# Decode attention with a gated MLP on one core: shorter ScalarE and VectorE programs, and the last weight load cut 16/8/5/2/1

## The chip, the cores and the metric

The kernel runs on one core of a Trainium2 chip. The metric is the time of one execution on the device in microseconds (us), and smaller is better. The profile's span, from the first to the last instruction, is 1.3 to 1.8 us shorter than that time in the runs of this case.

## The reference

One token attends to a cache of 16,384 keys and values in 32 heads, and a gate mixes the result with a small MLP branch.

```python
g = sigmoid((x * gate_w).sum(-1))                    # x: 1 x 512
q = x @ wq                                           # 32 heads of 128; wq: 512 x 4096
p = softmax(q @ k_cache.T * 128 ** -0.5)             # k_cache: 32 x 16384 x 128, bfloat16
a = (p @ v_cache).reshape(1, 4096) @ wo              # v_cache as k_cache; wo: 4096 x 512
b = (z1 * (w_sp * layernorm(z2) + b_sp)) @ w_out     # z1, z2: halves of gelu(x @ w_in)
return g * a + (1 - g) * b
```

The two caches are 2 x 134.2 MB. Everything else is 11 MB. Each byte is used once.

## The kernel before

Heads are handled in pairs. The whole program hangs on one queue of loads, issued by SyncE (SP) into three buffers of 64 KB per partition in SBUF, the memory next to the engines: wq, w_in and w_out first, then K0, K1, V0, K2, V1, K3, ... V15, then wo.

```python
    k_at = [max(2 * i - 1, 0) for i in range(NP)]          # place of K of pair i in the sequence
    v_at = [min(2 * i + 2, 2 * NP - 1) for i in range(NP)]
    ...
    for n, kind, i in loads:                               # a load waits for its buffer's last user
        wait = [user[n - 3]] if n >= 3 else [w_free] if buf[n % 3] is setup else []
        ...
            sp.op(lambda e, ...: e.dma_start(out=buf[n % 3][...], in_=src[...]), wait=..., inc=(done, 16))
    for j, (a, b) in enumerate(zip(WO_CUTS[:-1], WO_CUTS[1:])):
        sp.op(lambda e, a=a, b=b: e.dma_start(out=wo[:, a * D:b * D], in_=wo_src[:, a * D:b * D]),
              wait=[user[wo_at - 3]] if a == 0 else (), inc=(ld_o[j], 16))
```

For a pair, VectorE (DVE) multiplies K by q, TensorE (PE) adds over the head dimension, DVE finishes the scores, and ScalarE (ACT) takes the exponentials. That frees K's buffer. PE then multiplies V by p, which frees V's.

```python
    def act_pairs(e):
        e.wait_ge(*p_zero)
        exps(e, 0)                       # exps: wait for the scores, two activations
        exps(e, 1)
        with e.Fori(2, NP) as i:
            renew(e)                     # drain PE's sums of an earlier pair, zero the bank
            exps(e, i)
        renew(e)
        ...
```

In the tail the sums are normalized and multiplied by wo: rows 0 to 15 (of 32 per partition) in a loop of four rows, the rest unrolled as the pieces of wo land.

```python
WO_CUTS = (0, 16, 24, 28, 31, 32)
...
    dve.op(lambda e: e.reciprocal(out=rl[:, :], in_=l_ps[:, 0:H]), wait=[(sl_s, 1)], mark=True)
    dve.chain(lambda e: e.tensor_scalar(out=rl, in0=rl, scalar1=g_sb[:, 0:1], ..., op0=ALU.mult, ...))
    o_ok = dve.chain(lambda e: e.tensor_tensor(out=o_sb, in0=o_ps[:, 0:H], in1=rl, op=ALU.mult),
                     wait=[used_v[-1]])
    ...
    for j, (a, b) in enumerate(zip(WO_CUTS[:-1], WO_CUTS[1:])):
        for k in range(max(a, WIDE), b):                   # WIDE = 16
            y_ok = add(o2[:, k:k + 1], wo[:, k * D:(k + 1) * D], [(ld_o[j], 16)] if k == a else (), ...)
        if b == 24:
            add(ones_f[:, 0:1], d_sb[:, :], [w_ok])        # the sum of rows 0 to 15
    # then: copy to SBUF on DVE and ACT, and the DMA of the output
```

The softmax here doesn't subtract the row's maximum and nothing guards it: scores larger than these inputs give would overflow.

## Time and profile before

| | before |
|---|---|
| median of the first three runs | 652.02 us (651.7 to 652.5) |
| span of the profiled run | 650.2 us |
| bytes on the load queue | 279.58 MB, 99.6% of 16 engines' span |
| one 64 KB packet, median of 3,840 | 2.422 us |
| last semaphore of wo's last row | 648.19 us |

The page of the kernel before, its parts 1 to 3 and 4. Part 1 has busy time, share and instructions of each engine; part 2 gives 40 slices of the span; part 3 gives each DMA queue's packets, MB and share of 16 engines' time; part 4 follows the chain that ended last.

```profile
...
PE 424.3 (65%) x2474; PEld 47.0 (7%) x1312; DVE 335.8 (52%) x159; ACT 45.8 (7%) x112; POOL 2.2 (0%) x10
...
GB/s 384 463 419 452 452 395 443 452 443 395 452 452 395 443 452 448 391 452 452 403 435 452 448 391 452 452 431 407 452 452 395 443 452 439 399 435 468 392 428 342
...
q1 hardware_dynamic: 6194, 279.58, 99.6%
q8 instruction: 1, 0.02, 0.0%
...
DMA 4%; SPq 0%; PE 0%; issue 0%; DVE 0%; ACT 0%; ACTq 0%
...
```

No compute engine is busy for more than 65% of the span, and the load queue is busy for 99.6%. That is how a kernel that waits for its bytes reads. The slices, but for the last, swing between 384 and 468 GB/s, since packets of 64 KB are counted whole, where they begin; long stretches are steadier. These are windows of the kernel before; columns are the stretch, its length, busy us (count) of PE, weight loads, DVE, ACT and Pool, the granted clock, the DMA share and GB/s:

```profile
...
40.00:600.00 560.00, 372.78 (x2118) 34.89 (x1069) 307.80 (x122) 32.93 (x89) 0.00 (x0) 0.84 1.00 433
...
647.25:650.20 2.95, 1.19 (x18) 0.50 (x14) 0.41 (x1) 0.36 (x1) 0.00 (x0) 1.00 0.08 24
...
```

The stream runs at 433 GB/s in the middle and is over at 647.25 us, but for 24 GB/s x 2.95 us of stragglers. A 64 KB packet takes 2.422 us, so 16 engines move 16 x 65,536 / 2.422 us = 433 GB/s: the engines are back to back. The Trainium skill, "DMA: Bandwidth & Descriptors", section "Where 436 GB/s comes from", derives a ceiling of 435 GB/s for the fabric, and the measured rate agrees with it; the same section says that the HBM side, at about 358 GB/s, binds loads from HBM, but this trace, of one core alone, shows 433. 279.58 MB at 433 GB/s are 645.7 us of the 650.2.

The rest is the end. These are the last lines of the timeline of the kernel before (start, duration, engine, line, operation, operands, count, and in brackets the idle time before and its releaser):

```profile
...
646.72 0.16 PEld L716 LDWEIGHTS ps_all<-d_sb,const-float32-1.0 128*1 128x1 f32 x4
...
647.02 0.52 PEld L716 LDWEIGHTS ps_all<-bufs,o 128*1 128x1 bf16 x8
...
647.94 0.38 PEld L716 LDWEIGHTS ps_all<-bufs,o 128*1 128x1 bf16 x8 [0.40 <-DMA bufs<-in_A_wo_dram]
...
648.61 0.41 DVE L731 CAST res<-ps_all 1x256 bf16<-1x256 f32 x1 [6.07 <-PE ps_all L716]
...
```

PE finishes the 4-row piece and is idle for 0.40 us until the 3-row piece lands. The 6 matmuls of that piece and the 2 of the last row follow without a wait in between that this view shows. The trace's events of semaphores (counters by which a finished transfer releases the engine that waits for it) are finer: the last row's sixteenth increment came at 648.19 us, and its first weights load at 648.23. (The timeline merges the two stretches because the gap is too short.) The result copy and the output DMA end the kernel.

ACT's timeline of the kernel before:

```profile
...
63.96 1.28 ACT L592 ACT_TABLE_LOAD   x1 [29.56 <-ACTq L86]
65.26 0.42 ACT L592 ACTIVATE p_t<-s_sb 64x256 bf16<-64x256 f32 x1
...
```

The activation table for Exp (1.28 us) is loaded in front of the first exponentials, and K2's load is issued when the first half of them is done.

### The profile page before, as it was taken

Reading aid. Unit: us, or ns where it says so; the run is one execution under the profiler, and the core shown is the slowest. Engines: PE = TensorE matmul, PEld = TensorE weight load, DVE = VectorE, ACT = ScalarE, POOL = GpSimd, SP = SyncE. Lnnn points to the kernel's source line nnn. Section 1 sums busy time; section 2 is a strip of 40 time slices with the busy share of each in tenths; the row PEclk is TensorE's granted clock in tenths of the full one; section 3 lists DMA queues with packets and bytes.
Section 4 is the critical chain, followed back from the end, with each engine's and each line's share of the span. In section 5 each row is a group of like instructions: output and inputs, shape, how many; then the busy total and the mean of one; then the engine's idle time right before and its main releaser. Section 6 shows DMA issues by size and latency. Waiting matters only on the chain. (4 is left out here: it accounts for less than half of the span.)

```text
span 650.2 us, 7753 instructions
## 1 busy us (share of the span) xinstructions
PE 424.3 (65%) x2474; PEld 47.0 (7%) x1312; DVE 335.8 (52%) x159; ACT 45.8 (7%) x112; POOL 2.2 (0%) x10
## 2 busy tenths in 40 slices
PE   0646687847477574857757486584748857478678
PEld 0000000000101000010000101000010100001022
DVE  3457839256380835628165370835628174465600
ACT  2210000100001000010100001000000100001011
POOL 1000000000000000000000000000000000000000
PEclk9959798958889796888969679796977969698979
DMA  9999999999999999999999999999999999999998
GB/s 384 463 419 452 452 395 443 452 443 395 452 452 395 443 452 448 391 452 452 403 435 452 448 391 452 452 431 407 452 452 395 443 452 439 399 435 468 392 428 342
DMA packets 6203, 279.60 MB, mean 430 GB/s; under 512 B 695, under 2 KB 826, under 8 KB 1210
## 3 DMA queue, kind: packets, MB, share of 16 engines
q1 hardware_dynamic: 6194, 279.58, 99.6%
q8 instruction: 1, 0.02, 0.0%
q10 hardware_dynamic: 8, 0.00, 0.0%
HBM read 279.58 MB, written 0.00 MB: 430 GB/s over the span
## 5 line engine op out<-in xcount | busy, mean ns | idle before, releaser
L579 DVE TENSOR_TENSOR bufs<-bufs,qb x64 | 281.4, 4418 | 170.8 <-DVEq L86 170.8
L91 PE MATMUL ps_all<-bufs,ident 128*128 x960 | 258.8, 423 | 0.0
L496 PE MATMUL ps_all<-bufs,ident 128*128 x64 | 28.6, 446 | 154.2 <-PEq L86 153.9
L106 PE MATMUL ps_all<-bufs,p_t 128*8 x1024 | 82.5, 396 | 30.1 <-PEq L86 20.1
L564 DVE TENSOR_REDUCE s_sb<-ps_all 128x64 f32<-128x512 f32 x64 | 44.0, 687 | 93.1 <-DVEq L86 93.1
L91 PE MATMUL ps_all<-zero,ident 128*8 128x512 bf16 (+2 forms) x167 | 59.5, 388 | 0.0
L592 ACT ACTIVATE p_t<-s_sb 64x256 f32 (+1 forms) x32 | 13.3, 415 | 433.1 <-ACTq L86 432.7
L496 PEld LDWEIGHTS ps_all<-bufs,ident 128*128 128x128 bf16 x64 | 6.3, 99 | 365.6 <-issue 365.6
L106 PEld LDWEIGHTS ps_all<-bufs,p_t 128*8 x1024 | 19.4, 83 | 163.1 <-issue 161.6
L531 PE MATMUL ps_all<-pick,d_sb 128*128 128x2 f32 x128 | 17.0, 255 | 16.5 <-PEq L86 16.5
L531 PEld LDWEIGHTS ps_all<-pick,d_sb 128*128 128x128 f32 x128 | 15.7, 193 | 34.7 <-issue 34.7
L601 ACT COPY d_sb<-ps_all 128x512 f32<-128x512 f32 x16 | 9.4, 586 | 105.4 <-ACTq L86 105.4
L606 ACT CAST ps_all<-zero 128x512 f32<-128x512 bf16 x15 | 8.8, 589 | 1.7
L666 DVE RECIPROCAL rl<-ps_all 128x32 f32<-128x32 f32 x1 | 0.4, 357 | 12.2 <-PE ps_all L552 12.2
L381 DVE TENSOR_TENSOR bufs<-ps_all,ident 128x896 f32<-128x896 f32 x2 | 2.1, 1086 | 8.6 <-PE ps_all L91 8.6
L669 DVE TENSOR_TENSOR o_sb<-ps_all,rl 128x32 bf16<-128x32 f32 x1 | 0.2, 191 | 11.5 <-PE ps_all L531 11.5
L592 ACT ACTIVATION_READ_ACCUMULATOR p_t<-s_sb (+1 forms) x32 | 5.9, 185 | 0.0
L321 PE MATMUL ps_all<-xgw,const-float32-1.0 1*128 1x3 f32 x2 | 0.6, 360 | 8.0 <-DVE xgw L317 8.0
L91 PE MATMUL ps_all<-bufs,xb 128*128 x12 | 5.0, 552 | 0.0
L106 PE MATMUL ps_all<-bufs,u 128*1 x14 | 2.6, 372 | 3.1 <-ACT ps_all L427 2.4
L345 PE MATMUL ps_all<-bufs,xb 128*128 x4 | 2.3, 574 | 3.3 <-DMA bufs<-in_B_w_in_dram 3.3
L106 PE MATMUL ps_all<-bufs,xb 128*64 x32 | 3.6, 380 | 0.0
(76 smaller groups left out, 40.2 us busy)
## 6 DMA issues: line engine op xcount, KB each, us to landing
bufs<-in_A_k_cache_dram SPq DMA_DIRECT2D x2, 4096.0 KB, 36.2
bufs<-in_A_v_cache_dram SPq DMA_DIRECT2D x1, 5120.0 KB, 34.5
bufs<-in_A_wq_dram SPq DMA_DIRECT2D x1, 4096.0 KB, 12.3
bufs<-in_A_v_cache_dram SPq DMA_DIRECT2D x1, 2048.0 KB, 39.0
bufs<-in_A_wo_dram SPq DMA_DIRECT2D x1, 2048.0 KB, 25.4
bufs<-in_B_w_in_dram SPq DMA_DIRECT2D x1, 1792.0 KB, 15.5
bufs<-in_A_v_cache_dram SPq DMA_DIRECT2D x1, 1024.0 KB, 41.0
bufs<-in_A_wo_dram SPq DMA_DIRECT2D x1, 1024.0 KB, 27.6
```

Of the source, the lines that this page charges most:

```text
L91: ins = eng.matmul(out, lhsT=lhsT, rhs=rhs, **flags).ins
L106: ins = eng.matmul(bank[0:m, 0:n], lhsT=lhsT, rhs=rhs, **flags).ins
L321: g_ok = pe.op(lambda e: e.matmul(g_ps, lhsT=ones_f[0:1, :], rhs=xgw[:, :], start=True, stop=True), wait=[xgw_ok], mark=True)
L345: if n else matmul_on(nc, e, lambda: e.matmul(args[0], lhsT=args[1], rhs=args[2], **flags), [at, (xa, 0)]))
L381: dve.op(lambda e, h=h, zh=zh: e.tensor_tensor(out=zm[:, 2 * h * ZB:2 * (h + 1) * ZB].rearrange("p (b m k) -> p b m k", b=2, k=FhC), in0=z ...
L496: matmul_on(nc, e, lambda: e.matmul(s3, lhsT=ident[:, :], rhs=k3[:, :, 0:W], start=True, **flags), [(kw, 0)])
L531: ins = e.matmul(o2, lhsT=d_sb[:, r * Dh:(r + 1) * Dh], rhs=pick[:, r * 2:(r + 1) * 2], start=False, stop=False, skip_group_check=True)
L564: return e.tensor_reduce(out=s_sb[:, c * QK:(c + 1) * QK], in_=s_ps[c % 2].rearrange("p (j w) -> p j w", w=W), axis=AX.X, op=ALU.add)
L579: e.tensor_tensor(out=k3, in0=k3, in1=qi, op=ALU.mult).then_inc(mul_s, 1)
L592: e.activation(out=p_t[rows, bass.ds(at, NG * 8)].rearrange("p (t c) -> p t c", c=8)[:, :, 4 * s:4 * s + 4], in_=s_sb[rows, :].rearrange(" ...
L601: return e.copy(out=d_sb[:, :], in_=d_ps)
L606: e.copy(out=d_ps, in_=zero[:, :]).then_inc(drn_s, 1)
```

## The change

The intent: the ScalarE and VectorE programs are shortened, by emitting the exponentials once in a loop of branches and by merging steps of the set-up and of the tail. The last pieces of wo become 5/2/1 rows instead of 4/3/1. The core of the diff:

```diff
-WO_CUTS = (0, 16, 24, 28, 31, 32)
+WO_CUTS = (0, 16, 24, 29, 31, 32)
...
-    for t in [L_sb, p_t, zero]:
+    for t in [sel, L_sb, p_t, zero]:
         p_zero = pool.op(lambda e, t=t: e.memset(t[:, :], 0.0), mark=True)
+    sel_ok = (pool.sem, ident_ok[1] + 1)
-    const_ok = dve.op(lambda e: e.memset(sel[:, :], 0.0), mark=True)
...
-    dve.op(lambda e: e.tensor_copy(out=wbf[:, :], in_=g_ps[:, 1:3]), wait=[gm_ok], mark=True)
-    g_free = dve.chain(lambda e: e.memset(g_ps, 0.0))
+    wbf_ok = act.op(lambda e: e.copy(out=wbf[:, :], in_=g_ps[:, 1:3]), mark=True)
+    g_free = dve.op(lambda e: e.memset(g_ps, 0.0), wait=[wbf_ok], mark=True)
...
     def act_pairs(e):
+        i = counter(e, "ia", 0)
         e.wait_ge(*p_zero)
-        exps(e, 0)
-        exps(e, 1)
-        with e.Fori(2, NP) as i:
+        e.activation(out=var[:, :], in_=eps_t[:, :], func=ACT.Exp)
+        nc.br("act_exps", engines=kind)
+        with nc.body("act_renew", valid_engines=kind):
             renew(e)
-            exps(e, i)
+            nc.br("act_exps", engines=kind)
+        with nc.body("act_exps", valid_engines=kind):
+            exps(e, value(e, i, NP - 1))
+            e.reg_alu(i, i, 1, ALU.add)
+            e.br_lt(i, 2, on_true="act_exps", on_false="act_more")
+        with nc.body("act_more", valid_engines=kind):
+            e.br_lt(i, NP, on_true="act_renew", on_false="act_last")
...
-    dve.chain(lambda e: e.tensor_scalar(out=rl[:, :], in0=rl[:, :], scalar1=g_sb[:, 0:1],
-                                        scalar2=0.0, op0=ALU.mult, op1=ALU.add))
-    o_ok = dve.chain(lambda e: e.tensor_tensor(out=o_sb[:, :], in0=o_ps[:, 0:H], in1=rl[:, :],
-                                               op=ALU.mult), wait=[used_v[-1]])
+    o_ok = dve.chain(lambda e: e.scalar_tensor_tensor(
+        out=o_sb[:, :], in0=o_ps[:, 0:H], scalar=g_sb[:, 0:1], in1=rl[:, :], op0=ALU.mult,
+        op1=ALU.mult), wait=[used_v[-1]])
```

More of the change, by code (lines that the diff above doesn't have):

```diff
@@ L307, in gated_mix_kernel @@
         out=sel[:, :].rearrange("h (i x) -> h i x", x=P + 1)[:, :, 0:P:4],
-        in_=ident[0:H, 0:H].unsqueeze(1).broadcast_to([H, 4, H])), wait=[const_ok, ident_ok],
+        in_=ident[0:H, 0:H].unsqueeze(1).broadcast_to([H, 4, H])), wait=[sel_ok],
         mark=True)
@@ L314, in gated_mix_kernel @@
     dve.op(lambda e: e.tensor_tensor(out=xg_row[:, :], in0=x_row[:, :], in1=gw_row[:, :],
-                                     op=ALU.mult), wait=[(ld_x, 16), (ld_g, 48)], mark=True)
+                                     op=ALU.mult), wait=[(ld_g, 48)], mark=True)
     dve.op(lambda e: e.tensor_copy(out=xgw[:, 1:3], in_=wb_row[:, :]), mark=True)
@@ L324, in gated_mix_kernel @@
            wait=[g_ok], mark=True)
-    gm_ok = act.op(lambda e: e.activation(out=gm_sb[:, :], in_=g_ps[:, 0:1], func=ACT.Sigmoid,
+    act.op(lambda e: e.activation(out=gm_sb[:, :], in_=g_ps[:, 0:1], func=ACT.Sigmoid,
                                           scale=-1.0), mark=True)
-    dve.op(lambda e: e.tensor_copy(out=wbf[:, :], in_=g_ps[:, 1:3]), wait=[gm_ok], mark=True)
-    g_free = dve.chain(lambda e: e.memset(g_ps, 0.0))
+    wbf_ok = act.op(lambda e: e.copy(out=wbf[:, :], in_=g_ps[:, 1:3]), mark=True)
+    g_free = dve.op(lambda e: e.memset(g_ps, 0.0), wait=[wbf_ok], mark=True)
     def pe_gmlp(e):
@@ L608, in act_pairs @@
     def act_pairs(e):
+        kind = [e.engine]
+        i = counter(e, "ia", 0)
         e.wait_ge(*p_zero)
-        exps(e, 0)
-        exps(e, 1)
-        with e.Fori(2, NP) as i:
+        e.activation(out=var[:, :], in_=eps_t[:, :], func=ACT.Exp)
+        nc.br("act_exps", engines=kind)
+        with nc.body("act_renew", valid_engines=kind):
             renew(e)
-            exps(e, i)
+            nc.br("act_exps", engines=kind)
[5 more added lines that the diff above has]
+            e.br_lt(i, NP, on_true="act_renew", on_false="act_last")
+        nc.switch_bb("act_last")
         renew(e)
```

## The prediction

> **What bounds the kernel.** The load stream. The page's queue part gives 279.58 MB on one hardware queue, filling 99.6% of 16 engines' span. In the trace a 64 KB packet takes 2.422 us (median of 3,840), so 16 engines move 65,536 x 16 / 2.422 = 433 GB/s; the windows view shows the same from 40 to 600 us. The Trainium skill, "DMA: Bandwidth & Descriptors", section "Where 436 GB/s comes from", puts the fabric's ceiling at 435 GB/s; the trace agrees. Counting packets in flight, no stretch over 30 ns has fewer than 14 of 16 engines busy between 2.9 and 647.3 us. So 279.58 MB / 433 GB/s = 646 us is fixed by bytes that the change does not touch. About 4 to 5 us at the two ends are left. Compute engines are far below (page, part 1: PE 65%, DVE 52%, ACT 7%).
>
> **What the change does.**
> 1. Set-up. DVE loses the memset of sel (0.27 us) and the copy of wbf (0.16); Pool gains a memset of about 0.3 us and ACT a copy of about 0.2 us (estimates from those). All lie before 17.1 us, where PE waits for w_in's DMA. Worth nothing.
> 2. ScalarE loop. The exponentials are emitted once, not three times; each round adds a compare-and-branch (0.04 us in the trace). A dummy exponential moves the 1.28 us table load from 64.0 us, in front of the first exponentials, to about 34 us. K2's load is issued 1.3 us sooner, but by 65.8 us 31.8 MB had been asked for and about 28 moved (estimate from 433 GB/s): the queue was not empty. Later whole loads take 31 to 41 us from issue to landing (page, part 6) against 19.4 us of their own, so 0.1 us later costs nothing.
> 3. Tail, VectorE. Scale and multiply become one fused multiply: 0.24 us less at 629 us, where 11.5 us of slack follow; the fused one may take 0.05 us more than 0.19 at 641.2 us. PE catches up with the loads after that. Worth nothing.
> 4. wo pieces. The 3-row piece's semaphore comes at 647.91 us and PE resumes at 647.94; the last row's comes at 648.20, its weights load at 648.23. So the last row's landing sets the end already. With 5/2/1 PE has 4 matmuls instead of 6 before the last row, and waits for the same row. Worth 0 to 0.05 us.
> 5. Program length. One 16,384-byte instruction fetch (1.1 us) falls at 647.3 us, amid the last row's stragglers. The Trainium skill, "Runtime: NRT & Kernel Launch", section "Instruction fetch mechanics", says that refills come in 16 KiB blocks; the trace agrees in size. If a shorter program keeps it out of the tail, up to 0.3 us comes off the last landing: one chance in three.
>
> On the critical path: about 0.1 us of 652.
>
> **Prediction.** 651.9 us, range 651.0 to 652.8. Chances: faster by over 2% 0.005, within 2% 0.99, slower 0.005.
>
> **What would show it.** Right: DMA share above 99%, a 64 KB packet at 2.42 us, the chain ending in wo's last pieces, PE, one copy, the output; the table load near 34 us. Step 4 wrong: over 0.1 us between the last row's landing and its matmul, before or after. Step 5 right: no instruction packet, or elsewhere, and a sooner last landing.
>
> **What would make it wrong.** A load issued late because the branch loop delays a buffer's release (a gap in the DMA share); a semaphore or branch stall that the trace of before cannot show; a chip whose stream is slower.

## More of the kernel before

SP's timeline of the kernel before:

```profile
...
65.79 0.33 SPq L638 DMA_DIRECT2D bufs<-in_A_k_cache_dram  x1
90.87 0.33 SPq L638 DMA_DIRECT2D bufs<-in_A_v_cache_dram  x1
```

The line of 90.87 us is V1's load, issued when the first half of the second pair's exponentials is done and K1's buffer is free.

## The result, and the profile after

| | before | after |
|---|---|---|
| median of 6 runs | 651.68 us (651.54 to 652.5) | 651.58 us (651.44 to 653.31) |
| ratio | | 1.0002, 95% interval 0.9989 to 1.0015 |
| span of the profiled run | 650.2 us | 650.2 us |
| wo's last semaphore | 648.19 us | 648.19 us |

The ratio is the mean time of one kernel's fast runs over that of the other's in the same rounds, so it is not quite the ratio of the medians. Here one run of 653.31 us lifts the mean of after while its median is 0.10 us lower.

The page of the kernel after, from the same parts:

```profile
...
PE 423.5 (65%) x2474; PEld 47.0 (7%) x1312; DVE 335.2 (52%) x156; ACT 46.1 (7%) x114; POOL 2.6 (0%) x11
...
q1 hardware_dynamic: 6194, 279.58, 99.6%
q8 instruction: 1, 0.02, 0.0%
...
PE 0%; DVE 0%; issue 0%
...
```

PE is busy for 423.5 us instead of 424.3, DVE for 335.2 instead of 335.8 and ACT for 46.1 instead of 45.8. The load queue has the same bytes and share. Part 4 looks different: before, the chain hung on the DMA of wo, and now it names only PE and DVE. That is a matter of attribution, as the tail shows. Windows of the kernel after:

```profile
...
40.00:600.00 560.00, 372.21 (x2118) 35.16 (x1069) 307.84 (x122) 31.64 (x88) 0.00 (x0) 0.84 1.00 433
...
647.25:650.20 2.95, 1.26 (x18) 0.52 (x16) 0.41 (x1) 0.36 (x1) 0.00 (x0) 1.00 0.05 17
...
```

The end of its timeline:

```profile
...
646.76 0.17 PEld L724 LDWEIGHTS ps_all<-d_sb,const-float32-1.0 128*1 128x1 f32 x4
...
647.28 0.42 PEld L724 LDWEIGHTS ps_all<-bufs,o 128*1 128x1 bf16 x10 [0.36 <-DMA bufs<-in_A_wo_dram]
...
647.96 0.09 PEld L724 LDWEIGHTS ps_all<-bufs,o 128*1 128x1 bf16 x4 [0.26 <-DMA bufs<-in_A_wo_dram]
648.23 0.08 PEld L724 LDWEIGHTS ps_all<-bufs,o 128*1 128x1 bf16 x2 [0.19 <-DMA bufs<-in_A_wo_dram]
...
648.58 0.41 DVE L739 CAST res<-ps_all 1x256 bf16<-1x256 f32 x1 [6.04 <-PE ps_all L724]
...
```

PE stops for the DMA of wo three times after row 24: before the 5-row piece (0.36 us), the 2-row piece (0.26 us) and the last row (0.19 us). The kernel waits for the last landing as before. The followed chain stayed on PE, probably because the matmuls, whose ends are modelled, overlap these waits. From the last semaphore to the copy it is 648.58 - 648.19 = 0.39 us, against 0.42 us before: a gain of 0.03 us.

The other moves of the change, in the kernel after: the early table load and the first exponentials on ACT, the loads that they release on SP, and the fused multiply in DVE's tail, one timeline each.

```profile
...
34.39 1.28 ACT L612 ACT_TABLE_LOAD   x1
35.69 0.20 ACT L612 ACTIVATE var<-eps_t 128x1 f32<-128x1 f32 x1
64.11 0.42 ACT L592 ACTIVATE p_t<-s_sb 64x256 f32 x1 [28.22 <-ACTq L86]
...
```

```profile
...
64.65 0.33 SPq L647 DMA_DIRECT2D bufs<-in_A_k_cache_dram  x1
90.98 0.33 SPq L647 DMA_DIRECT2D bufs<-in_A_v_cache_dram  x1
```

```profile
...
641.17 0.25 DVE L676 SCALAR_TENSOR_TENSOR o_sb<-ps_all,g_sb,rl 128x32 bf16<-128x32 f32 x1 [11.75 <-PE ps_all L531]
...
```

The table load is 29.6 us earlier, and K2's load 1.14 us (64.65 against 65.79). V1's load, one pair later, is not earlier at all (90.98 against 90.87), because the second pair's exponentials wait for the scores. The fused multiply takes 0.25 us. Before, it was 0.24 us for the scaling, long before it was needed, and 0.19 us for the multiply.

### The profile page after: what moved, and what is told of

Its sections match the earlier page's. It is cut to its first block, busy times and chain, and to the rows that moved or that the text cites. A ratio compares the mean times of both kernels' runs of the same rounds, so it can differ in the third digit from the quotient of the medians.

```text
span 650.2 us, 7779 instructions
## 1 busy us (share of the span) xinstructions
PE 423.5 (65%) x2474; PEld 47.0 (7%) x1312; DVE 335.2 (52%) x156; ACT 46.1 (7%) x114; POOL 2.6 (0%) x11
## 5 line engine op out<-in xcount | busy, mean ns | idle before, releaser
L592 ACT ACTIVATE p_t<-s_sb 64x256 f32 x32 | 13.3, 414 | 462.5 <-ACTq L86 462.1
L676 DVE SCALAR_TENSOR_TENSOR o_sb<-ps_all,g_sb,rl 128x32 bf16<-128x32 f32 x1 | 0.3, 251 | 11.7 <-PE ps_all L531 11.7
L592 ACT ACTIVATION_READ_ACCUMULATOR p_t<-s_sb x32 | 5.9, 185 | 0.0
L301 DVE MEMSET ps_all<- 128x3584 f32 x1 | 3.0, 3045 | 1.9 <-PEq L770 1.9
## 6 DMA issues: line engine op xcount, KB each, us to landing
bufs<-in_A_wo_dram SPq DMA_DIRECT2D x1, 2048.0 KB, 25.5
```

The source lines that it names most:

```text
L301: dve.op(lambda e: e.memset(ps_all[:, 0:7 * 512], 0.0), mark=True)
L592: e.activation(out=p_t[rows, bass.ds(at, NG * 8)].rearrange("p (t c) -> p t c", c=8)[:, :, 4 * s:4 * s + 4], in_=s_sb[rows, :].rearrange(" ...
```

## The experiments

Twelve runs of eleven kernels were made, each run a single look beside the kernel before on the same chip (651.54, 652.13 and 651.55 us in the three calls). All passed the comparison with the reference.

Where I speak of "the slowest engine", I read the trace's packet records: a load of 128 packets of 64 KB is spread over 16 DMA engines, and the end of its last packet is the slowest engine's. The Trainium skill, "DMA: Bandwidth & Descriptors", section "Why a DMA increments its semaphore by 16 and not by 1", says that each engine adds its own increment and only the full 16 means that all data has landed. The traces agree: in the kernel after, the last two increments for wo come at 648.19 us, over 0.2 us behind all others, and PE's last weights load at 648.23.

### The cuts alone

```diff
 (on the kernel before)
-WO_CUTS = (0, 16, 24, 28, 31, 32)
+WO_CUTS = (0, 16, 24, 29, 31, 32)
```

> Before, with only the wo cuts of the change (rows 16/8/5/2/1). Theory (the last landing sets the end, and the bytes in front of it are the same): PE stops three times for a wo piece after row 24, at about 647.3, 647.95 and 648.2 us, as in the changed kernel; the last row's weights load at 648.2 us and the result copy starts at 648.55 to 648.62 us, within 0.05 us of before's 648.61. Rival (fewer matmuls behind the next to last landing shorten the tail): the copy starts 0.1 us or more before 648.61.

The end of this kernel's timeline:

```profile
...
648.06 0.09 PEld L716 LDWEIGHTS ps_all<-bufs,o 128*1 128x1 bf16 x4 [0.23 <-DMA bufs<-in_A_wo_dram]
648.35 0.08 PEld L716 LDWEIGHTS ps_all<-bufs,o 128*1 128x1 bf16 x2 [0.21 <-DMA bufs<-in_A_wo_dram]
...
648.70 0.41 DVE L731 CAST res<-ps_all 1x256 bf16<-1x256 f32 x1 [6.04 <-PE ps_all L716]
...
```

The span was 650.3 us. PE stopped for the last two pieces as in the kernel after, but the copy started at 648.70 us, which is outside the stated range on the late side. The reason is that the last semaphore came at 648.31 us, 0.12 us later than in the other two. The cuts did not cause that: the slowest engine of this look was already 0.11 us behind the kernel after at the end of K0's load (37.86 against 37.74 us). The time from the last semaphore to the copy was 0.39 us again. The rival, a copy 0.1 us earlier than before's, is out. The cuts are worth 0.03 us behind the landing, and the landing itself moves more than that from one look to the next.

### Four rows in the last piece

```diff
 (on the kernel after)
-WO_CUTS = (0, 16, 24, 29, 31, 32)
+WO_CUTS = (0, 16, 24, 28, 32)
```

> The changed kernel with wo in four pieces of 16/8/4/4 rows: 8 matmuls instead of 2 hang on the last landing. Theory: the last landing stays at about 648.2 us, since the bytes are the same, and the end moves by the 6 more matmuls: in before 8 matmuls took 0.65 us to the copy, in the changed kernel 2 took 0.35 us, so the copy starts 0.30 us later, at about 648.9 us, and the span is about 650.5 us. Rival (the cuts do not matter at all, or fewer pieces land sooner): the copy starts at 648.6 us or earlier.

The end of this kernel's timeline:

```profile
...
648.49 0.31 PEld L724 LDWEIGHTS ps_all<-bufs,o 128*1 128x1 bf16 x8 [0.78 <-DMA bufs<-in_A_wo_dram]
...
649.16 0.41 DVE L739 CAST res<-ps_all 1x256 bf16<-1x256 f32 x1 [6.50 <-PE ps_all L724]
...
```

The span was 650.8 us. The last semaphore came at 648.44 us and the copy started at 649.16, so 0.72 us lie behind the landing instead of 0.39. The 6 matmuls more cost 0.33 us; 0.30 had been expected. The landing itself was 0.25 us later, which I had not expected. About half of it (0.09 us at K0's load, 0.13 at V14's) is a lateness that the slowest engine carried through the whole stream; the rest one look does not explain. So the cuts do matter in the direction that the theory says. With one row in the last piece, both kernels already had the least that whole rows allow, and 3 against 2 rows in the piece before it are hidden by the wait for the last row.

### A later VectorE in the tail

```diff
 (on the kernel after)
+    dve.op(lambda e: e.memset(junk[:, :], 0.0), wait=[used_v[-1]])
     o_ok = dve.chain(lambda e: e.scalar_tensor_tensor(
```

> The changed kernel with a 128x512 memset on VectorE (about 0.3 to 0.5 us) between the last pair's sums and the fused multiply, several times the 0.06 us by which the fused multiply is longer than the plain one. Theory (VectorE's tail is off the path, since PE waits for the wo pieces behind it): o_sb comes 0.3 to 0.5 us later, PE's wait of 0.36 us in front of the 5-row piece shrinks to about nothing, the last row's weights still load at 648.2 us and the copy starts within 0.1 us of 648.58. Rival (the tail from o_sb on is one chain): the copy starts 0.3 to 0.5 us later.

The memset took 0.48 us, and the last operand for wo on DVE came 0.31 us later (642.65 against 642.34 us). The span was 650.1 us, and the copy started at 648.52 us. The rival is out: 0.31 us, five times what the fused multiply costs, change nothing. One detail of the expectation was wrong. PE's wait before the 5-row piece did not shrink (0.35 us), since the loop over the first 16 rows began at 643.30 us, against 643.38 in the kernel after. That fits the landing of wo's first piece, 25.5 us after its issue at 617.6, so even the loop did not wait for DVE.

### A much slower ScalarE loop

```diff
 (on the kernel after)
         with nc.body("act_exps", valid_engines=kind):
+            for _ in range(4):
+                e.copy(out=junk[:, :], in_=zero[:, :]).then_inc(junk_s, 1)
+                take(e, junk_s)
             exps(e, value(e, i, NP - 1))
```

> The changed kernel with four 128x512 copies (0.59 us each, about 2.6 us with their waits) put in front of every pair's exponentials on ScalarE: 16 x 2.6 = 42 us of work, 26 times the compare-and-branch that the change adds, on the same chain that frees the buffers. Theory (the queue of loads is never empty): the K loads are issued about 2.6 us later and land after a correspondingly shorter time from their issue, no gap in the stream, span within 0.3 us of 650.2. Rival (the ScalarE loop is on the chain that releases the loads): the span grows by a good part of 42 us, at least 5 us.

This kernel's window from 40 to 600 us, and two pieces of its ScalarE timeline:

```profile
...
40.00:600.00 560.00, 375.44 (x2116) 34.63 (x1069) 307.64 (x122) 67.72 (x148) 0.00 (x0) 0.84 1.00 433
...
```

```profile
...
316.55 0.42 ACT L594 ACTIVATE p_t<-s_sb 64x256 f32 x1 [28.65 <-ACTq L86]
...
324.92 2.81 ACT L621 CAST junk<-zero 128x512 f32<-128x512 bf16 x4
```

The span was 650.1 us, the rate from 40 to 600 us was again 433 GB/s, and no gap appeared. ScalarE's busy time in that window rose from 31.64 to 67.72 us. But the loads hardly came later: exponentials that stood at 316.12 us in the kernel after stood at 316.55 us here. The four copies (2.81 us, at 324.92) are done in ScalarE's idle time, before the scores are ready. So the run shows that ScalarE's loop has room for 2.8 us per pair. It does not show how much later a load may be issued, because it did not delay one by 2.6 us as I had meant it to.

### Fewer bytes

```diff
 (on the kernel after; a quarter version has (0, 3 * KP // 4))
+        if kind == "k" and i == 5:
+            cuts = (0, KP // 2)
         for a, b, done in zip(cuts[:-1], cuts[1:], sems):
```

Both versions leave old data in a part of the buffer and so do not compute the reference; the comparison still passed them, so its tolerance does not see a part of one K load among sixteen.

> The changed kernel with one of the sixteen K loads cut to its first half (4.19 MB less; the result is wrong on purpose, the engines' work is the same). Theory (bytes over 433 GB/s set the time): the span falls by 4.19 MB / 433 GB/s = 9.7 us, to about 640.5 us. Rival (the engines' chain through a pair is about as long as its loads, so fewer bytes only make room): the span falls by less than 5 us.

The span was 642.3 us: 7.9 us less, not 9.7. The rival bound of 5 us is passed, but the theory is off by 1.8 us. The trace shows where most of it went. V4's load is the one issued after the short load. Without a hole its packets would have begun 9.69 us earlier than the 211.19 us of the kernel after, at 201.50, but it was issued only at 201.36 us, and its first packet began at 202.31. V4's issue on SP in the kernel after, and in this run:

```profile
...
200.57 0.33 SPq L647 DMA_DIRECT2D bufs<-in_A_v_cache_dram  x1
...
```

```profile
...
201.36 0.33 SPq L649 DMA_DIRECT2D bufs<-in_A_v_cache_dram  x1
...
```

Windows of this run show that no large packet began between 201 and 202 us:

```profile
...
201.00:202.00 1.00, 0.91 (x17) 0.14 (x8) 0.00 (x0) 0.84 (x4) 0.00 (x0) 1.00 0.01 0
202.00:203.00 1.00, 0.87 (x17) 0.14 (x8) 0.05 (x1) 0.00 (x0) 0.00 (x0) 1.00 2.63 918
...
```

A window counts a packet where it begins, so its zero is not yet a stop. By the packet records the engines finished the short load between 201.65 and 202.12 us and began V4's between 202.31 and 203.08, so that, taken in this order, each stood for 0.7 to 1.0 us. The first packets begin 0.8 us late, and slower packets took most of the rest: 2.94 us in the mean for V4's first sixteen and 2.45 us from 261 to 320 us, instead of 2.42. So the queue's margin is finite. In the kernel after V4 was issued at 200.57 us and its packets began at 211.19 us. A load needs 0.95 us from its issue to its first packet when the queue is empty (201.36 to 202.31), which leaves 211.19 - 200.57 - 0.95 = 9.7 us. A cut of 9.7 us uses it up, and the issue, 0.8 us later in this look, did the rest.

> The changed kernel with one of the sixteen K loads cut to its first three quarters (2.10 MB less; wrong on purpose). In the run with half a load gone the span fell by 7.9 us of the expected 9.7, with a gap of 1.2 us in the stream after the short load. Theory (bytes over 433 GB/s set the time, and the queue holds about 10 us of other loads when a V load is issued): 4.84 us less queued leaves no gap, and the span falls by 4.84 us, to 645.4 us within 0.2. Rival (the engines' chain takes back part of any gain): it falls by less than 4.3 us.

(The gap of 1.2 us in that text is the 0.7 to 1.0 us per engine above.) With a quarter gone the span was 645.3 us, 4.9 us less, and no hole appeared; loads after the short one began 4.8 us earlier to the end. Below the margin, time is bytes over rate. The rival is out.

### Padding PE's program

```diff
 (on the kernel after; 160 in the second version)
+    for _ in range(80):
+        pe.raw(lambda e: e.nop().then_inc(pad_s, 1))      # ahead of PE's first matmul
```

> The changed kernel with 80 idle semaphore instructions at the start of PE's program (283 instructions, 18,112 bytes, become 363). Theory (the instruction fetch at 647.2 us is PE's, made where its program reaches a 16 KiB block's end, and it holds up the last wo rows on the DMA engine it uses): the fetch comes several us before 647 us, the last row's packets end sooner, its weights load at 647.9 to 648.05 us instead of 648.23, and the span is 0.2 to 0.3 us shorter. Rival 1 (the fetch belongs to another engine): it stays at about 647.2 us. Rival 2 (the fetch is PE's but harmless): it moves, and the last row's weights still load at about 648.2 us.

The end of the timeline with 80 instructions:

```profile
...
646.81 0.74 PEld L727 LDWEIGHTS ps_all<-bufs,o 128*1 128x1 bf16 x16 [1.10 <-DMA bufs<-in_A_wo_dram]
...
648.38 0.41 PEld L727 LDWEIGHTS ps_all<-bufs,o 128*1 128x1 bf16 x10 [0.61 <-DMA bufs<-in_A_wo_dram]
...
649.35 0.08 PEld L727 LDWEIGHTS ps_all<-bufs,o 128*1 128x1 bf16 x2 [0.24 <-DMA bufs<-in_A_wo_dram]
649.69 0.41 DVE L742 CAST res<-ps_all 1x256 bf16<-1x256 f32 x1 [7.28 <-PE ps_all L727]
...
```

The fetch moved from 647.22 to 643.83 us, so it is PE's. The lengths of ScalarE's and VectorE's programs, which the change shortened, have nothing to do with it. But the rest of my theory was upside down: the span grew to 651.3 us. PE now waited 1.10 us for the second piece of wo, which had kept it waiting for nothing before, and the last semaphore came at 649.31 us instead of 648.19. The stream thinned out at 647.2 us as ever, and the last data packet ended at 648.88 us instead of 647.76. The fetch took 1.08 us on one DMA engine that still had loads to move. That engine was 1.1 us late from then on, and each later piece waited for it. The late start of PE is not the cause: the last load of 64 KB packets, V14's, still ended 0.1 us earlier than in the kernel after (618.21 against 618.29 us). In the kernels before and after the same fetch falls at 647.3 and 647.2 us, as the engines run out of work (in the kernel after, 13 packets were in flight at 647.25 us and 4 at 647.5).

> The changed kernel with 160 instead of 80 idle semaphore instructions at the start of PE's program. Theory (PE fetches 16 KiB where its program passes a block's end, and a fetch while the stream is full makes one DMA engine about 1.1 us late, which every later load then waits for): the fetch comes hundreds of us earlier, in a loop that PE enters in the first 100 us, and the last landing is again about 1.1 us later than in the changed kernel, span 651.2 to 651.4 us. Rival (the late engine of the 80 instruction run was an accident, or the delay came from the late start of PE): span 650.2 within 0.3, or, for the late start, more than 2 us longer.

The span was 653.6 us: more than the theory's 651.2 to 651.4, and on the side of the rival's late start. The trace keeps the two apart by time. The fetch came at 49.47 us. The load under way then (K1's) ended 1.2 us later than in the kernel after, by the slowest engine alone (8 packets before the end of a load the difference was 0.05 us), and the next two loads kept that lateness: 1.19 and 1.18 us. That is the theory's effect. Then the rival's came on top. PE's late start had pushed V1's issue to 97.21 us. The stream thinned out from 95.4 us on and was empty from 96.95 to 98.17 us, and the load after the hole ended 3.5 us late, now on all engines. In the hole the lateness of the one engine vanished, since all restarted together. So the same run shows both a fetch that made one engine 1.2 us late, and the place where the kernel has the least room.

### Padding ScalarE's program

```diff
 (on the kernel after)
+    for _ in range(200):
+        act.raw(lambda e: e.nop().then_inc(pad_s, 1))     # ahead of the first sigmoid
```

> The changed kernel with 200 idle semaphore instructions in ScalarE's idle time before the first sigmoid (86 instructions, 5,504 bytes, become 286, 18,304 bytes). Theory (an engine fetches once its program passes 16 KiB, so the few instructions that the change takes away at 5.5 KB change nothing): a second instruction packet of 16,384 bytes appears, and PE's stays at about 647.2 us. Rival (the fetches do not depend on the engine's program length): still one packet. In both the span stays at 650.2 us within 0.5 us, or grows by ScalarE's delay if the 200 take longer than its 8.9 us of idle time.

The span was 652.2 us, which neither side had expected. The 200 instructions did take longer than the idle time (the first sigmoid came at 17.75 us instead of 13.92), but ScalarE's next step came at 29.04 us instead of 28.93, so this delay is not the 2 us. A second queue of instruction packets appeared beside PE's: two of 8,192 bytes, at 10.47 and 18.71 us. (In the other traces this queue, q14, has such packets only outside the span.) K0's load, under way then, ended 1.0 us later than in the kernel after, by the slowest engine alone. The rest came in stretches of slow packets between 92 and 98 us (up to 3.5 us instead of 2.42), after which that engine was 1.9 us late. In this run V1 was issued at 93.69 us, 2.7 us later than in the kernel after, with the queue nearly dry. PE's fetch stood at 649.17 us, later along with the late pieces of wo.

> The same kernel as the run with 200 idle instructions on ScalarE, whose span was 2.0 us longer, with two extra instruction packets of 8 KB (0.31 us each) at 10 and 19 us and a stretch of slow packets at 92 to 97 us. Theory (the fetches cost their DMA engine at most 0.62 us, the rest was the slow stretch, which is not the kernel's): the two packets come again at the same places, and the span is 650.2 to 650.9 us. Rival (the 200 instructions cost the 2 us): the span is again about 652.2 us.

The instruction queues of this run's page (packets, MB, share of 16 engines):

```profile
...
q8 instruction: 1, 0.02, 0.0%
q14 instruction: 2, 0.02, 0.0%
...
```

The same kernel again had a span of 650.8 us, inside the theory's range. The two packets came at 10.10 and 20.75 us, K0's load ended 0.63 us late by its slowest engine, and that lateness stayed between 0.63 and 0.67 us through the remaining loads. So the fetches, or what came with them, cost 0.6 to 1.0 us, and they cost it for good. The other 1.0 us of the first look is not the 200 instructions by themselves. That it came from V1's later issue fits the times but is not separated from chance.

### A shorter PE program

```diff
 (on the kernel after)
-WIDE = 16
+WIDE = 24
-        if b == 24:
+        if b == 29:
```

> The changed kernel with rows 16 to 23 of wo multiplied in PE's loop of four rows (24 rows in the loop instead of 16) and the loop's sum added after the 5-row piece: PE's program falls from 283 instructions (18,112 bytes) to 251 (16,064 bytes). Theory (program length decides): no instruction packet at all if PE's block holds 256 of the kernel's own instructions, otherwise one after 647.5 us; with none, the last row's weights load by 648.05 us and the span is 0.1 to 0.3 us shorter. Rival (fetch harmless): the last row's weights load at 648.2 us or later.

The end of this kernel's timeline:

```profile
...
648.38 0.09 PEld L724 LDWEIGHTS ps_all<-d_sb,const-float32-1.0 128*1 128x1 f32 x4 [0.38 <-ACT d_sb L719]
...
648.60 0.41 PEld L724 LDWEIGHTS ps_all<-bufs,o 128*1 128x1 bf16 x6
...
649.38 0.41 DVE L739 CAST res<-ps_all 1x256 bf16<-1x256 f32 x1 [6.73 <-PE ps_all L724]
...
```

PE's program fell to 251 instructions, and its fetch came at 648.99 us, after all data. The last semaphore came at 648.33 us, not earlier than in the kernels with the fetch at 647.2 (648.06 to 648.32 in six looks). Of the 0.14 us by which it is later than the kernel after's 648.19, 0.12 us are a lateness of the slowest engine that came up during V1's load and was still there at V14's; so the landing is the same within 0.02 us. The kernel after's own increments agree: the two slowest engines were 0.27 us behind the others at the 5-row piece, whose last increments came at 647.23 and 647.24 us, just as the fetch began, and 0.23 us behind at the last row. So the fetch at 647.2 us does not hold up the last landing, and the rival is right. The span grew to 651.0 us for another reason: the copy of the loop's sum now ends later, PE waits for it (0.38 us), and the last rows' weights load at 648.60 us, behind the sum instead of on their landing.

### The kernel after once more

> The changed kernel once more, unaltered, for the spread of one look. Span 650.2 within 0.3 us, the last row's weights load at 648.1 to 648.4 us, the instruction packet at 647.2 to 647.4 us, no gap in the stream.

The span was 650.3 us, and the last row's weights loaded at 648.37 us, with no gap; the instruction packet came at 647.18 us, 0.02 us outside the stated stretch. The slowest engine's end of the first 64 KB load was 0.10 us later than in the first look, and the same 0.10 to 0.13 us at every later load and at the last semaphore. The slowed ScalarE run had it 0.30 us earlier at the first load and kept that too. So most of the small scatter of spans, 650.1 to 650.3 us, is there before 38 us, in what one DMA engine loses by then. Not all lateness begins there: in the run with the shorter PE program the slowest engine was 0.12 us early up to K2's load and 0.23 us late after V1's, the load with the least room. What takes the time is open in both places.

## Why the prediction was right

- **The bound.** The stream sets the time, as predicted. A quarter of a K load less gives 4.9 us less, against 4.84 from bytes over rate. The measured median of 651.58 us is 0.3 us below the predicted 651.9 and inside its range. The 0.3 us are the base's: I had 652.02 us from three runs of the kernel before, and six gave 651.68. That the medians then differ by just the 0.1 us that I had forecast is luck, since the interval of the ratio, 0.9989 to 1.0015, is 1.7 us wide.
- **1, set-up: worth nothing.** Right. PE's first matmul on w_in starts at 17.17 us, after 17.13 before, and V0's load is issued at 36.20 us, after 36.23.
- **2, the ScalarE loop: off the path.** Right in outcome: 2.8 us per pair instead of 0.04 us change nothing. The support that I gave was too generous. "31 to 41 us from issue to landing against 19.4 us of their own" suggests 11.7 us of room and holds roughly for a median V load: it measured 9.7 us for V4, and 9.1 to 10.3 for V2 to V13 of the kernel after, once the 0.95 us of start is taken off. (By the sizes of the loads, 32.1 MB had been asked for by 65.8 us, not 31.8; that changes nothing.) It does not hold for V1, whose packets began at 95.10 us in the kernel before after an issue at 90.87: 95.10 - 90.87 - 0.95 = 3.3 us. An issue at 93.69 us went with slow packets, and one at 97.21 us left a hole.
- **3, the tail on VectorE: worth nothing.** Right: the fused multiply cost 0.06 us more, and 0.31 us more were also hidden.
- **4, the wo pieces: 0 to 0.05 us.** Right, 0.03 us. The step that I named as what would show it wrong, over 0.1 us between the last landing and its matmul, did not occur (0.04 us in both).
- **5, program length: up to 0.3 us, one chance in three.** The chance did not come, and the reasoning was wrong twice. The fetch belongs to PE, whose program the change did not shorten, and in the tail it holds up nothing. Where it does cost time, 0.6 to 1.2 us, is earlier, while the stream is full.
- **The chain.** I expected it to end in wo's last pieces by name. It named PE alone, although PE's waits are still ended by those pieces.

No experiment points to a version that beats both kernels by an amount that could be measured. The stream begins at 1.0 us and thins out at 647.2 us, and what the change addressed lies outside of these 646 us.

## What to carry to other kernels

When one queue of loads is full from the first microsecond to the last, read every planned saving against that queue: instructions saved beside it are worth nothing until they change when a load is issued or what hangs on the last landing. Ask for the margin of each load separately, as the time at which its packets begin minus its issue (and minus the 0.95 us that a load takes to start), and look for the smallest one, because medians hide a load that is nearly late, here V1 with 3.3 us. And look at where instruction fetches fall: the same 16 KB cost nothing as the stream ran out, and about a microsecond while it was full, kept until the stream next stopped or ended.

## What the Trainium skill lacked or had wrong

- "Runtime: NRT & Kernel Launch", section "Instruction fetch mechanics", calls the cost of crossing a 16 KiB boundary "mostly hidden". Neither it nor another page says what a fetch costs loads that share its DMA engine. While the stream was full, one fetch of 16,384 bytes took 1.05 and 1.08 us in two runs, and one engine was 1.1 to 1.2 us late for the loads after it.
- The same section says that refills come in 16 KiB blocks. PE's did (one packet of 16,384 bytes in each of the 14 traces); ScalarE's came as two packets of 8,192 bytes, some 8 to 11 us apart, once its program had grown to 18,304 bytes.
- "DMA: Bandwidth & Descriptors" does not say that one engine's lateness lasts: a difference of 0.1 to 0.7 us in the slowest engine's first 64 KB load was still there, within 0.05 us, at the last one 580 us later, in seven runs whose stream was not disturbed in between. Around V1's load, at 95 to 117 us, lateness came up anew in two runs, and a hole in the stream wiped it out in a third.
- The same page, section "Specifications", gives about 600 ns as the first byte latency of loads issued from SyncE. From the start of the issue to the start of the first packet it was 0.95 and 0.96 us in the two cases with an empty queue, and 0.62 to 0.63 us from the end of the issue's 0.33 us, so the figure agrees if it is counted from there.
